# An attention layer with two expert layers: part-by-part order in every batch, ropes moved and cut, loads moved

## The chip, the cores and the metric

The kernel runs on one core of a Trainium2 chip. The metric is device time in microseconds (us), the median of the runs. A core has five engines with queues of their own, each executed in order: TensorE (PE; its weight loads are listed apart as PEld), VectorE (DVE), ScalarE (ACT), GpSimd (POOL) and the sync engine (SP), which here only issues DMAs.

## The reference

Four batches, eight heads, 576 positions, head size 64. After a rotation of q and k (the rope), scores, softmax and the product with v, the heads are laid side by side, and two expert layers follow: the first takes the maximum of three products and multiplies it by an output matrix, the second is a silu layer of width 2048.

```python
def rotate(x):
    x1, x2 = (x[..., :half], x[..., half:])
    return np.concatenate([x1 * cos - x2 * sin, x1 * sin + x2 * cos], axis=-1)
q_rot, k_rot = (rotate(q), rotate(k))
scores = scale * np.matmul(q_rot, k_rot.transpose(0, 1, 3, 2))
scores = scores - np.max(scores, axis=-1, keepdims=True)
attn = np.exp(scores)
attn = attn / (np.sum(attn, axis=-1, keepdims=True) + 1e-09)
attn_out = np.matmul(attn, v)
...
x = np.ascontiguousarray(attn_out.transpose(0, 2, 1, 3)).reshape(B * S, H * D)
h = np.maximum(np.maximum(x @ w1, x @ w2), x @ w3)
x = h @ w_out
h = x @ w_in
out = (h * (1.0 / (1.0 + np.exp(-h)))) @ w_out2
```

## The kernel before

**Attention tiles.** Heads are taken in pairs, four per batch. The 576 queries of a pair are five tiles: four of 128 rows and one of 64. `PARTS` calls tiles 0 and 1 the first part (256 queries) and tiles 2 to 4 the second (320). So there are 80 tiles, and the list `order` gives their sequence. In the first batch it goes through all four pairs' first parts and then through their second parts; in the other three it takes pair by pair, all five tiles of one before the next. A tile goes through scores on TensorE (lines 352 and 355), the negated row maximum on VectorE (362), exp on ScalarE (369), sum and reciprocal (379, 380), scaling on ScalarE (382), nine transposes on TensorE (398) with copies by ScalarE or VectorE (402, 404), and after each part of a pair the product with v (`av`, lines 413 and 417), which writes that pair's rows of x (420, 421).

**What comes ahead of a pair.** Its q and k are loaded into one of three raw buffers (`load_qk`), rotated in place (`qk_rope`: three instructions, lines 309, 310 and 313, with one work buffer w), and transposed (`qk_turn`, line 323), after which the raw buffer is free. A table `events` hangs these steps on tile numbers: `first[b, hp]` is a pair's first tile, and loads, ropes and turns stand so many tiles ahead of it. The rope of the first batch's pairs 0 and 1 is VectorE's, all others are GpSimd's.

**Filler.** The first expert layer (`moe1`, its matmuls in `group`, line 482) is a generator that the loop over the tiles draws on, some 8000 columns per tile. A batch is 576 matmuls of line 482: for each part 18 groups of 12 ("up") and 4 groups of 18 ("down"), with 256 columns in the first part and 320 in the second. `x_ready` says from which tile on a part of x may be used: the part must be whole for all four pairs. The last batch's matmuls come after the loop over the tiles, and the second expert layer after them. In the same loop the weights are made ready: W1's and WO1's pieces are loaded, narrowed (208, 210, 219, 220), measured, scaled and split in a high and a low half (`split`: GpSimd's line 155 and VectorE's 158, alternating piece by piece), and the second layer's weights are narrowed 256 columns at a time (205, 206, 219, 220).

**What sets the order.** The program order above is a priority; a scheduler with a timeline of its own then fixes every engine's queue, so instructions may move ahead of others. On the chip each queue runs in the fixed order.

## Time and profile before

| | us |
|---|---|
| median of 3 runs | 1127.57 (1127.56 to 1130.81) |
| the profiled execution | 1126.39 |
| its span, first to last instruction | 1124.7 |
| TensorE busy | 1036.1 |
| VectorE, ScalarE, GpSimd busy | 584.1, 503.9, 238.7 |
| mean granted TensorE clock | 0.956 |

The attention runs from the first row maximum at 23.9 us to the last at 651.8; the second expert layer fills the time from about 736 us to the end. TensorE's busy time includes waits between pipelined matmuls, so a stretch in which it is busy throughout is only known to have no visible gap.

### The profile page before, as it was taken

The page shows a single profiled execution, that of the slowest core. Times are in us where ns is not written, and L with a number is a line of the kernel's source. Part 1 is how long each engine was busy: PE and PEld are TensorE (multiplying, and loading weights), DVE is VectorE, ACT ScalarE, POOL GpSimd, SP SyncE. Part 2 cuts the span into 40 slices and gives each one's busy share as a digit, 9 for nine tenths or more (in the row PEclk, how much of TensorE's full clock was granted, in tenths as well). Part 3 has the DMA queues.
Part 4 walks back from the last instruction along what each step waited for, and adds up shares of the span by engine and source line. Part 5 has one row for each costly group of instructions (what it writes and reads, how often), then busy time and mean ns, then how long its engine had stood idle before and what let it go on. Part 6 is the DMA issues. An engine that isn't in the chain of part 4 may idle for free.

```text
span 1124.7 us, 16293 instructions
## 1 busy us (share of the span) xinstructions
PE 1036.1 (92%) x6250; PEld 632.7 (56%) x6250; DVE 584.1 (52%) x1102; ACT 503.9 (45%) x1200; POOL 238.7 (21%) x189
## 2 busy tenths in 40 slices
PE   2477898999978999999999997999999999999997
PEld 2244574666646776656776666654444444444554
DVE  4967667444477656566756549623444213423322
ACT  3567685555766676666767632121212002202111
POOL 3875113112134414332211106300000000000000
PEclk9687797899988999999999999999999999999999
DMA  7633021102332342232233136000101010100000
GB/s 191 187 106 116 17 68 51 51 2 59 98 102 87 107 121 86 60 96 71 85 92 93 54 131 264 15 24 1 38 29 47 13 26 1 29 29 1 19 20 19
DMA packets 79390, 76.10 MB, mean 68 GB/s; under 512 B 44752, under 2 KB 61648, under 8 KB 78288
## 3 DMA queue, kind: packets, MB, share of 16 engines
q1 hardware_dynamic: 75760, 65.03, 19.3%
q10 hardware_dynamic: 3552, 10.03, 2.7%
q8 instruction: 49, 0.80, 0.3%
q14 instruction: 29, 0.24, 0.1%
HBM read 57.21 MB, written 17.83 MB: 67 GB/s over the span
## 4 chain that ended last, share of the span: by engine, by line
PE 78%; DVE 5%; issue 2%; POOL 2%; ACT 2%; DMA 1%; SPq 0%; DVEq 0%; POOLq 0%; ACTq 0%
PE m L482 39%; PE o L726 17%; PE s L355 7%; PE tr L398 6%; PE xp L417 5%; PE s L352 2%; PE xp L413 1%; POOL wi L155 1%; DVE wi L158 1%; PE tr L323 1%; DVE z L219 1%; ACT e L382 1%; DVE nb L362 0%; DMA yr<-yscr 0%; POOL z L206 0%
## 5 line engine op out<-in xcount | busy, mean ns | idle before, releaser
L482 PE MATMUL m<-x,w 128*128 128x320 f16 (+1 forms) x1632 | 232.3, 290 | 9.1 <-DVE t L500 2.6
L726 PE MATMUL o<-wo,g 128*128 128x512 f16 x828 | 193.2, 379 | 0.0
L482 PEld LDWEIGHTS <-w 128*128 128x128 f16 x1632 | 157.5, 99 | 62.6 <-issue 20.9
L482 PE MATMUL m<-yt,wi 128*128 128x512 f16 (+1 forms) x920 | 189.8, 358 | 0.0
L712 ACT ACTIVATE gt<-m,ch 128x512 f32<-128x512 f32 (+1 forms) x80 | 51.5, 644 | 297.0 <-PE m L482 282.7
L362 DVE TENSOR_REDUCE nb<-s 128x2 f32<-128x1152 f32 (+1 forms) x80 | 108.2, 1352 | 64.8 <-PE s L355 64.7
L726 PEld LDWEIGHTS <-g 128*128 128x128 f16 x864 | 84.5, 98 | 99.7
L482 PEld LDWEIGHTS <-wi 128*128 128x128 f16 x920 | 89.6, 98 | 89.4
L369 ACT ACTIVATE e<-s,nb 128x576 f32<-128x576 f32 (+1 forms) x160 | 116.6, 734 | 50.6 <-DVE nb L362 49.6
L398 PE MATMUL tr<-ident,e 128*128 128x128 f32 (+1 forms) x720 | 118.7, 287 | 20.0 <-ACT pt L402 9.5
L382 ACT ACTIVATE e<-e,rec 128x576 f32<-128x576 f32 (+1 forms) x160 | 115.0, 767 | 23.7 <-DVE rec L380 23.6
L157 DVE TENSOR_SCALAR g<-gt,sg 128x512 f16<-128x512 f32 (+1 forms) x80 | 36.7, 459 | 162.8 <-ACT gt L712 162.8
L398 PEld LDWEIGHTS tr<-ident,e 128*128 128x128 f32 (+1 forms) x720 | 84.1, 149 | 50.9 <-ACT pt L402 14.7
L355 PE MATMUL s<-T 64*128 64x512 f32 (+5 forms) x480 | 109.3, 531 | 0.0
L206 POOL TENSOR_SCALAR z<-z 128x256 uint16<-128x256 uint16 x64 | 53.4, 834 | 211.1 <-DVE z L205 208.9
L417 PE MATMUL xp<-pt,vd 128*64 128x256 f32 (+1 forms) x512 | 90.7, 433 | 0.0
L402 ACT ACTIVATE pt<-tr 128x384 f32<-128x384 f32 (+1 forms) x160 | 70.3, 453 | 41.8 <-PE tr L398 41.2
L355 PEld LDWEIGHTS s<-T 64*128 64x128 f32 (+1 forms) x480 | 56.3, 192 | 38.5 <-issue 19.6
L482 PE MATMUL m<-h,wo 128*128 128x256 f16 (+1 forms) x512 | 72.8, 287 | 0.0
L500 DVE SCALAR_TENSOR_TENSOR t<-m,t 128x256 f32<-128x256 f32 (+1 forms) x96 | 43.5, 454 | 50.0 <-PE m L482 44.9
L309 POOL TENSOR_TENSOR w<-qk,sin_sb 128x1152 f32<-128x1152 f32 x14 | 37.5, 2676 | 128.5 <-DMA qk<-in_k_dram 103.7
L417 PEld LDWEIGHTS xp<-pt,vd 128*64 128x64 f32 x512 | 38.4, 141 | 37.5 <-issue 21.1
(158 smaller groups left out, 1090.8 us busy)
## 6 DMA issues: line engine op xcount, KB each, us to landing
z<-in_moe_w_in_dram SPq DMA_DIRECT2D x32, 256.0 KB, 2.9
z<-in_moe_w_out_dram SPq DMA_DIRECT2D x32, 256.0 KB, 3.0
w<-in_moe_w_dram ACTq DMA_DIRECT2D x6, 768.0 KB, 7.7
wo<-in_moe_w_dram ACTq DMA_DIRECT2D x6, 768.0 KB, 4.8
qk<-in_q_dram SPq DMA_DIRECT2D x32, 128.0 KB, 3.2
qk<-in_k_dram SPq DMA_DIRECT2D x32, 128.0 KB, 3.1
vd<-in_v_dram SPq DMA_DIRECT2D x16, 256.0 KB, 2.8
zwi<-z SPq DMA_DIRECT2D x32, 128.0 KB, 2.9
```

The source lines that it names most:

```text
L206: nc.gpsimd.tensor_scalar(out=q[:, :, 2], in0=q[:, :, 1], scalar1=step, scalar2=off, op0=ALU.mult, op1=ALU.add)
L355: nc.tensor.matmul(s[0:n, o:o + m], qs[r], kt[r, a:a + m], start=True, stop=True)
L362: x = nc.vector.tensor_reduce(out=nb[0:n], in_=s[0:n, 0:1152].rearrange("p (h k) -> p h k", h=2), op=ALU.max, axis=AX.X, negate=True)
L369: x = nc.scalar.activation(out=e[0:n, HK[g]], in_=s[0:n, HK[g]], func=AF.Exp, bias=nb[0:n, g:g + 1], accum_out=sm[0:n, g:g + 1])
L382: nc.scalar.activation(out=e[0:n, HK[g]], in_=e[0:n, HK[g]], func=AF.Copy, scale=r[0:n, g:g + 1])
L398: nc.tensor.transpose(tr[:, i * n:(i + 1) * n], e[0:n, c * P:(c + 1) * P], ident[0:n, 0:n])
L402: nc.scalar.activation(out=to, in_=of, func=AF.Copy)
L417: nc.tensor.matmul(xp[r, 0:n], v4[:, g, c, :], pt[:, c + 5 * g, :], start=False, stop=(c == 3))
L482: nc.tensor.matmul(ps[:, 0:n], l, r, start=(i == 0), stop=(i == len(passes) - 1))
L500: nc.vector.scalar_tensor_tensor(out=t, in0=ps[:, 0:n], scalar=2.0 ** -22, in1=part[-1], op0=ALU.mult, op1=ALU.max)
L712: nc.scalar.activation(out=gt, in_=ps[:, 0:n], func=AF.Silu, scale=ch)
L726: nc.tensor.matmul(ps, l, r, start=(f == 0 and i == 0), stop=(f == NF2 - 1 and i == 2))
```

## The change

It has four edits. `order` goes through the first parts of all pairs and then the second parts in every batch, so a batch's first part of x is whole after 8 tiles instead of 17. With this the first tiles of a batch's pairs stand two tiles apart instead of five, and the loads, ropes and turns that hang on them come closer together: a batch's first pair is loaded 12 tiles ahead of its first tile, the fourth 7 tiles ahead of the third pair's first tile, and the ropes stand 6 tiles ahead instead of 5. In the first batch VectorE does all four ropes. A rope on GpSimd is done in three chunks of 6 of the 18 blocks of columns, nine instructions of 128x384 instead of three of 128x1152. And the third and fourth v loads of batches 2 and 3 come 4 tiles ahead of the batch. Line numbers after the rope are higher by 2 or 3 in the changed kernel.

```diff
--- before.py
+++ after.py
@@ -304,13 +304,16 @@
         t = raw_t[b, hp]
         w = w_p.tile([P, 18, D], F32, tag="w", name="w")
         tt = (eng or nc.gpsimd).tensor_tensor
-        t4, w4 = (x.rearrange("p (a h) d -> p a h d", h=2) for x in (t, w))
-        sin2, cos2 = (x.unsqueeze(2).to_broadcast([P, 9, 2, D]) for x in (sin_sb, cos_sb))
-        tt(out=w4, in0=t4, in1=sin2, op=ALU.mult)
-        tt(out=t4, in0=t4, in1=cos2, op=ALU.mult)
-        u4 = t.rearrange("p a (t e) -> p a t e", t=2)
-        w4 = w.rearrange("p a (t e) -> p a t e", t=2)
-        return tt(out=u4, in0=u4, in1=w4[:, :, ::-1, :], op=ALU.add)
+        for lo, hi in ((0, 18),) if eng else ((0, 6), (6, 12), (12, 18)):
+            r, v = t[:, lo:hi, :], w[:, lo:hi, :]
+            t4, w4 = (x.rearrange("p (a h) d -> p a h d", h=2) for x in (r, v))
+            sin2, cos2 = (x[:, lo // 2:hi // 2, :].unsqueeze(2).to_broadcast([P, (hi - lo) // 2, 2, D]) for x in (sin_sb, cos_sb))
+            tt(out=w4, in0=t4, in1=sin2, op=ALU.mult)
+            tt(out=t4, in0=t4, in1=cos2, op=ALU.mult)
+            u4 = r.rearrange("p a (t e) -> p a t e", t=2)
+            w4 = v.rearrange("p a (t e) -> p a t e", t=2)
+            x = tt(out=u4, in0=u4, in1=w4[:, :, ::-1, :], op=ALU.add)
+        return x
 
     def qk_turn(b, hp):
 
@@ -427,8 +430,7 @@
 
 
     PARTS = [(0, 256, (0, 1)), (256, 320, (2, 3, 4))]
-    order = [(0, hp, r) for r in range(2) for hp in range(NP)]
-    order += [(b, hp, r) for b in range(1, B) for hp in range(NP) for r in range(2)]
+    order = [(b, hp, r) for b in range(B) for r in range(2) for hp in range(NP)]
     tiles, events, first, x_ready = [], {}, {}, {}
 
     def at(j, f, *a):
@@ -442,15 +444,15 @@
     for i, (b, hp) in enumerate(pairs):
         u = first[b, hp]
         if i > 2:
-            at(first[pairs[i - 1]] - 9 if i != 4 else 8, load_qk, b, hp)
+            at(first[pairs[i - 1]] - (7 if hp == 3 else 9) if hp or i < 4 else first[b, hp] - 12, load_qk, b, hp)
         if i == 0:
             continue
-        at(u - 5 if i > 3 else i - 4, qk_rope, b, hp, nc.vector if i == 1 else None)
+        at(u - 6 if i > 3 else i - 4, qk_rope, b, hp, nc.vector if i < 4 else None)
         at(u - 3, qk_turn, b, hp)
     for b in range(1, B):
         u = first[b, 0]
         for hp in range(NP):
-            at(u - 10 + hp if hp < 2 or b > 1 else u - 4, load_v, b, hp)
+            at(u - 10 + hp if hp < 2 else u - 4, load_v, b, hp)
             at(u - 2, v_max, b, hp)
         at(u, v_scale, b)
```

TensorE's queue at batch 1, pair 3, tiles 37 and 38 of the program: s is the scores' tile, tr a transposed tile, qk a raw buffer, xp the product with v. Before:

```order
L352 MATMUL s_2839<-kd_0_115,T_2554 128x128
L355 MATMUL s_2839<-T_2554 128x512
L355 MATMUL s_2839<-T_2554 128x384
L355 MATMUL s_2839<-T_2554 128x128
L398 MATMUL tr_2866<-ident_78,e_2743 128x128 x3
L323 MATMUL tr_2884<-ident_78,qk_2097 128x128 x4
L329 MATMUL tr_2896<-ident_78,qk_2097 128x128
L323 MATMUL tr_2890<-ident_78,qk_2097 128x128 x4
L352 MATMUL s_2911<-kd_0_115,T_2554 128x128
L355 MATMUL s_2911<-T_2554 128x512
L355 MATMUL s_2911<-T_2554 128x384
L355 MATMUL s_2911<-T_2554 128x128
```

At the same place, from tile 35, after (x_2020 is batch 1's x, m a group of the expert layer):

```order
L401 MATMUL tr_2840<-ident_78,e_2637 128x64 x3
L355 MATMUL s_2819<-kd_0_114,T_1777 128x128
L358 MATMUL s_2819<-T_1777 128x512
L358 MATMUL s_2819<-T_1777 128x384
L358 MATMUL s_2819<-T_1777 128x128
L484 LDWEIGHTS w_0_127
L484 MATMUL m_2875<-x_2020,w_0_127 128x256
L484 LDWEIGHTS w_0_127
L484 MATMUL m_2875<-x_2020,w_0_127 128x256
L484 LDWEIGHTS w_0_127
L484 MATMUL m_2875<-x_2020,w_0_127 128x256
L484 LDWEIGHTS w_0_127
```

Between the scores of two tiles there stood transposes alone; now the up matmuls of batch 1 stand there.

TensorE's queue at tiles 77 and 78, the last pair of the last batch. Before, from tile 77's scores (x_3548 is batch 2's x):

```order
L352 MATMUL s_6451<-kd_0_115,T_6138 128x128
L355 MATMUL s_6451<-T_6138 128x512
L355 MATMUL s_6451<-T_6138 128x384
L355 MATMUL s_6451<-T_6138 128x128
L398 MATMUL tr_6472<-ident_78,e_6290 128x64 x3
L482 LDWEIGHTS w_0_127
L482 MATMUL m_6517<-x_3548,w_0_127 128x320
L482 LDWEIGHTS w_0_127
L482 MATMUL m_6517<-x_3548,w_0_127 128x320
L482 LDWEIGHTS w_0_127
L482 MATMUL m_6517<-x_3548,w_0_127 128x320
L482 LDWEIGHTS w_0_127
```

After, from tile 77's scores through tile 78's:

```order
L355 MATMUL s_6708<-kd_0_115,T_5531 128x128
L358 MATMUL s_6708<-T_5531 128x512
L358 MATMUL s_6708<-T_5531 128x384
L358 MATMUL s_6708<-T_5531 128x128
L401 MATMUL tr_6734<-ident_78,e_6566 128x128 x3
L401 MATMUL tr_6763<-ident_78,e_6629 128x64 x3
L401 MATMUL tr_6773<-ident_78,e_6629 128x64 x3
L401 MATMUL tr_6768<-ident_78,e_6629 128x64 x3
L355 MATMUL s_6747<-kd_0_115,T_5531 128x128
L358 MATMUL s_6747<-T_5531 128x512
L358 MATMUL s_6747<-T_5531 128x384
L358 MATMUL s_6747<-T_5531 128x128
```

The expert matmuls that stood between these scores have gone ahead of them.

VectorE's queue at the start (nb is the row maximum, w a piece of W1 on line 219 and 220, qk_173 and qk_218 the raw buffers of pairs 2 and 3). Before:

```order
L313 TENSOR_TENSOR qk_153<-qk_153,w_221 128x1152
L362 TENSOR_REDUCE nb_264<-s_259 128x2
L219 TENSOR_SCALAR w_0_127<-w_0_127 128x768 x2
L327 COPY T_229<-tr_236 128x512
L220 SCALAR_TENSOR_TENSOR w_0_127<-w_0_251,w_0_127 128x768
L220 SCALAR_TENSOR_TENSOR w_0_127<-w_1_253,w_0_127 128x768
```

After:

```order
L315 TENSOR_TENSOR qk_153<-qk_153,w_214 128x1152
L311 TENSOR_TENSOR w_225<-qk_173,sin_sb_111 128x1152
L312 TENSOR_TENSOR qk_173<-qk_173,cos_sb_110 128x1152
L315 TENSOR_TENSOR qk_173<-qk_173,w_225 128x1152
L365 TENSOR_REDUCE nb_264<-s_259 128x2
L219 TENSOR_SCALAR w_0_127<-w_0_127 128x768 x2
L330 COPY T_229<-tr_236 128x512
L336 COPY kd_0_113<-tr_242 64x64 x2
L311 TENSOR_TENSOR w_247<-qk_218,sin_sb_111 128x1152
L220 SCALAR_TENSOR_TENSOR w_0_127<-w_0_251,w_0_127 128x768
L220 SCALAR_TENSOR_TENSOR w_0_127<-w_1_253,w_0_127 128x768
```

Pair 2's rope now stands ahead of the first row maximum, and pair 3's begins ahead of the second.

GpSimd's queue at the end of the first batch (wo_0 and wo1f are WO1's pieces; qk_1720 and qk_1380 are batch 1's fourth pair, qk_2097 and qk_2312 batch 2's first). Before:

```order
L309 TENSOR_TENSOR w_2416<-qk_1720,sin_sb_111 128x1152
L310 TENSOR_TENSOR qk_1720<-qk_1720,cos_sb_110 128x1152
L313 TENSOR_TENSOR qk_1720<-qk_1720,w_2416 128x1152
L155 TENSOR_SCALAR wo1f_129<-wo_0_130,swo1s_1544 128x512
L155 TENSOR_SCALAR wo_0_130<-wo_0_130,swo1s_1544 128x512 x2
L155 TENSOR_SCALAR wo_0_130<-wo_0_130,swo1b_1550 128x512 x3
L309 TENSOR_TENSOR w_2767<-qk_2097,sin_sb_111 128x1152
L310 TENSOR_TENSOR qk_2097<-qk_2097,cos_sb_110 128x1152
```

After:

```order
L315 TENSOR_TENSOR qk_1380<-qk_1380,w_1678 128x384 x2
L155 TENSOR_SCALAR wo1f_129<-wo_0_130,swo1s_1595 128x512
L311 TENSOR_TENSOR w_2756<-qk_2312,sin_sb_111 128x384
L155 TENSOR_SCALAR wo_0_130<-wo_0_130,swo1s_1595 128x512
L312 TENSOR_TENSOR qk_2312<-qk_2312,cos_sb_110 128x384
L311 TENSOR_TENSOR w_2756<-qk_2312,sin_sb_111 128x384 x2
L315 TENSOR_TENSOR qk_2312<-qk_2312,w_2756 128x384
L155 TENSOR_SCALAR wo_0_130<-wo_0_130,swo1s_1595 128x512
L312 TENSOR_TENSOR qk_2312<-qk_2312,cos_sb_110 128x384 x2
L155 TENSOR_SCALAR wo_0_130<-wo_0_130,swo1b_1601 128x512
L315 TENSOR_TENSOR qk_2312<-qk_2312,w_2756 128x384 x2
L155 TENSOR_SCALAR wo_0_130<-wo_0_130,swo1b_1601 128x512
```

The ropes of batch 2's first pairs now stand between WO1's splits, where they followed the last one.

## Rows read from the trace of the kernel before

**Rows 1.** the page, 40 slices: busy tenths of TensorE, its granted clock
```profile
PE   2477898999978999999999997999999999999997
...
PEclk9687797899988999999999999999999999999999
```
**Rows 2.** stretches: us, busy us (x instructions) by engine, clock, DMA
```profile
298.30:346.10 47.80, 36.66 (x209) 22.37 (x207) 34.68 (x69) 32.52 (x90) 21.80 (x16) 0.86 0.41 114
346.10:497.60 151.50, 150.60 (x1070) 105.33 (x1069) 89.72 (x199) 99.54 (x262) 44.43 (x33) 0.99 0.30 88
```
**Rows 3.** the same view, line 482 alone (expert matmuls)
```profile
298.30:346.10 47.80, 2.49 (x14) 1.53 (x15) 0.86 0.41 114
346.10:497.60 151.50, 80.39 (x573) 53.99 (x571) 0.99 0.30 88
497.60:506.40 8.80, 0.29 (x2) 0.23 (x3) 0.82 0.44 136
506.40:651.60 145.20, 77.95 (x554) 52.52 (x552) 0.99 0.26 79
```
**Rows 4.** the same view, line 362 alone (row maxima)
```profile
298.30:346.10 47.80, 9.47 (x7) 0.86 0.41 114
346.10:497.60 151.50, 25.70 (x19) 0.99 0.30 88
...
506.40:651.60 145.20, 25.73 (x19) 0.99 0.26 79
```
**Rows 5.** timeline of TensorE: start, us, instruction, xcount, idle before and its end
```profile
312.06 0.58 PE L398 MATMUL tr<-ident,e 64*128 64x64 f32 x3 [2.41 <-ACT pt L402]
```
**Rows 6.** timeline of TensorE after the attention
```profile
702.99 1.91 PE L482 MATMUL m<-h,wo 128*128 128x256 f16 x16
...
714.25 19.05 PE L482 MATMUL m<-x,w 128*128 128x320 f16 x139
```
**Rows 7.** timeline of VectorE in the first hole
```profile
326.57 1.36 DVE L362 TENSOR_REDUCE nb<-s 128x2 f32<-128x1152 f32 x1
...
331.18 1.36 DVE L362 TENSOR_REDUCE nb<-s 128x2 f32<-128x1152 f32 x1 [0.38 <-PE s L355]
```
**Rows 8.** timeline of GpSimd in the first batch
```profile
33.45 2.64 POOL L309 TENSOR_TENSOR w<-qk,sin_sb 128x1152 f32<-128x1152 f32 x1 [2.37 <-DMA qk<-in_k_dram]
```
**Rows 9.** timeline of VectorE, GpSimd idle beside these three
```profile
13.08 1.36 DVE L309 TENSOR_TENSOR w<-qk,sin_sb 128x1152 f32<-128x1152 f32 x1 [11.91 <-DMA qk<-in_q_dram]
...
93.87 0.54 DVE L219 TENSOR_SCALAR w<-w 128x768 int32<-128x768 int32 x1
...
94.80 0.94 DVE L220 SCALAR_TENSOR_TENSOR w<-wo,w 128x768 int32<-128x768 int32 x1
```
**Rows 10.** groups of VectorE from 22 to 62 us
```profile
L219 DVE TENSOR_SCALAR w<-w 128x768 int32<-128x768 int32 x6 | 9.8, 1659 | 0.0
L220 DVE SCALAR_TENSOR_TENSOR w<-w,w 128x768 int32<-128x768 int32 x4 | 9.2, 2323 | 0.0
L220 DVE SCALAR_TENSOR_TENSOR w<-wo,w 128x768 int32<-128x768 int32 x2 | 5.1, 2579 | 0.0
```
**Rows 11.** timeline of GpSimd, then of VectorE, end of the first batch
```profile
177.83 2.63 POOL L309 TENSOR_TENSOR w<-qk,sin_sb 128x1152 f32<-128x1152 f32 x1 [4.47 <-DMA qk<-in_k_dram]
...
183.31 2.70 POOL L313 TENSOR_TENSOR qk<-qk,w 128x1152 f32<-128x1152 f32 x1
...
177.88 2.87 DVE L507 TENSOR_TENSOR h<-t,h 128x256 f16<-128x256 f32 x1
...
183.60 2.95 DVE L220 SCALAR_TENSOR_TENSOR wo<-w,wo 128x512 int32<-128x512 int32 x1
```
**Rows 12.** timeline of GpSimd: first and last WO1 split, the next rope
```profile
193.90 0.69 POOL L155 TENSOR_SCALAR wo1f<-wo,swo1s 128x512 f16<-128x512 f32 x1 [7.90 <-DVE swo1i L128]
...
204.46 0.69 POOL L155 TENSOR_SCALAR wo<-wo,swo1b 128x512 f16<-128x512 f32 x1 [2.89 <-DVE wo L158]
222.21 2.63 POOL L309 TENSOR_TENSOR w<-qk,sin_sb 128x1152 f32<-128x1152 f32 x1 [17.06 <-DMA qk<-in_k_dram]
```

## The prediction

> **What bounds the kernel now.** Read the slices of the span first: TensorE is at 9 tenths from slice 8 to the end, with 7 or 8 left in a few places, and its granted clock dips in the same places [rows 1]. So the kernel is TensorE's work plus the stretches in which it can't work. The dips are told apart by the table of stretches, cut where the row maxima of attention tiles begin (tile numbers count the 80 tiles in program order). From 298.3 to 346.1 us TensorE has 36.66 us busy of 47.80 at a clock of 0.86; behind it, from 346.1 to 497.6, it has 150.60 of 151.50 [rows 2]. The same stretches counted by line 482, the matmuls of the expert layer, say why: 573 and 554 of them lie in the two long stretches, 14 and 2 in the two holes [rows 3]. The count of row maxima gives the tiles: 19 in each long stretch, 7 in the first hole [rows 4], one in the second. In a hole TensorE waits for the steps of one tile's chain, 2.41 us for a copy of the transposed tile in the row shown, and nothing else is in its queue [rows 5]. The hole is there because batches 1 to 3 run head pair by head pair: the first part of x is whole only when the last pair's first two tiles are done, at tile 17 of 20, and by then the previous batch's expert matmuls have run out.
>
> **Price of a tile, filled and unfilled.** An expert matmul costs 1.91 - 0.27 us over 15 steps, 0.109 us, with 256 columns, and 19.05 us over 139, 0.137 us, with 320 [rows 6]; a batch has 288 of each, so 0.123 us on average. The filled stretches hold 296.7 us, 38 tiles and 1127 such matmuls (138.6 us): (296.7 - 138.6) / 38 = 4.16 us per attention tile. The holes hold 56.6 us, 8 tiles and 16 matmuls (2.0 us): 6.83 us per tile. A tile without filler therefore wastes 2.67 us, and a tile is full from about 2.67 / 0.123 = 22 expert matmuls upward. This includes what the low clock in the holes costs.
>
> **Part 1, the order part by part.** After the change x's first part is whole at tile 8 of each batch, and 9 tiles earlier than before. In the new order of TensorE's queue no tile from 24 to 74 is empty: tiles 33 to 39 get 18 to 36 expert matmuls each (10 in all seven before, by the order), tile 59 gets 36, and the leanest, with 9 to 13, stand between fuller ones. The 8 unfilled tiles go: 8 x 2.67 = -21.4 us. The matmuls that fill them come from later, and since total TensorE work stays, the filler has to run out somewhere: the last three tiles. The new order gives tiles 75 to 79 16, 12, 0, 0 and 24 expert matmuls, where before 23 to 26 stood in each. Against the 22 that fill a tile that wastes 0.7 + 1.2 + 2.7 + 2.7 + 0 = +7.3 us. Bounds of this term: the holes hold GpSimd's ropes, 21.80 us of its time in the first [rows 2], and the last tiles have none; the quickest bare tile took 4.61 us, from 326.57 to 331.18 [rows 7], and at that price two bare tiles waste 0.9 and all of them about +1; if tile 79 and the drain behind it are bare too, 5 x 2.7 = +13. I take 7.3. Sum of part 1: -14 us (-20 to -8). What the last batch leaves for after the attention, and the layer after it, is the same work as before, so it stays.
>
> **Part 2, four ropes by VectorE in the first batch.** GpSimd loses the ropes of head pairs 2 and 3, six instructions of some 2.64 us [rows 8]; VectorE gains six of 1.36 us [rows 9], +8.2 us on an engine that from 22 to 62 us has hardly a gap. But it isn't busy with its own work there. Line 219 takes 1.66 us on average and line 220 2.32 and 2.58 [rows 10], against 0.54 and 0.94 when GpSimd is idle [rows 9]: 6 x 1.12 + 4 x 1.38 + 2 x 1.64 = 15.5 us of waiting. Roughly 9 us of it lies beside the two ropes that leave. So the two sides cancel, +8.2 - 9, with one addition: VectorE runs in order, and rope 3 now stands ahead of the second tile's row maximum. Its data is there only at about 33.4 us, where GpSimd's rope 3 starts after waiting for that DMA [rows 8]; VectorE would come to it near 30, so up to 3 us idle, with the maxima of tiles 0 and 1, and so all scores behind them, queued behind. Against that, GpSimd's queue is 17 us shorter when the W1 splits need it. I take -1 us, from -7 (all waiting goes) to +8 (none goes).
>
> Here a rule of the Trainium skill speaks against the change. In our rows a line 220 that starts at 183.60, while a GpSimd rope instruction holds from 183.31 to 186.01, takes 2.95 us and ends half a us after it [rows 11]; its own time with 512 elements is some 0.63, two thirds of the 0.94 for 768 [rows 9]. It waits out the other instruction. The Trainium skill, page SBUF - State Buffer, section Who interferes with whom, says that a VectorE instruction with two SBUF inputs and a GpSimd instruction that reads SBUF share a port pair as an exclusive lock, and that the second one to start blocks until the first is through; the row agrees. By that rule VectorE's own ropes, with two SBUF inputs, block behind GpSimd's line-210 instructions as well, which still run from 36 us on at some 2 us each: three instructions of rope 3 at up to 2 us would add up to 6 us to this term, which the upper bound above already holds.
>
> **Part 3, GpSimd's ropes in three chunks.** A rope instruction of 2.7 us [rows 11] becomes three; linear in size each is 0.9 us, and as GpSimd's instruction of 0.69 us with 512 elements shows [rows 12] a fixed part must be small, so 0.9 to 1.1. Nine instead of three make a rope at most 2 us longer on an engine that is busy for 44.43 of the 151.50 us of the filled stretch [rows 2]. The gain is VectorE's shorter wait: at 178 to 187 us two instructions on the way to WO1's scale take 2.87 and 2.95 us [rows 11] where about 0.6 is their own time, 4.6 us too much; with waits cut to a third, -3. The cost is in the same place: the new GpSimd order puts 12 chunks between the first and the last of WO1's six splits, some 12 us, where before 7.1 us of gaps lay (193.90 to 205.15 with 6 x 0.69 busy) [rows 12]; the down product needs the last split, so up to +5. I take -1, from -4 to +7. In the filled stretches TensorE sets the pace and the shorter waits give nothing.
>
> **Part 4, loads.** q/k loads are issued 7, 9 or 12 tiles ahead; only the fourth pair of a batch is short, since its raw buffer comes free with the first pair's turn. In the first batch it lands before 177.83, when its rope starts now [rows 11], and is turned some 30 us later in the new order: 9 chunks of 1 us fit. Loads of v for batches 2 and 3 move behind the av products that free their buffers. Cost 0, hidden by 4 tiles of 6.8 us; without that cover the turn on TensorE would wait.
>
> **Sum.** -14 - 1 - 1 = -16 us against the profiled execution's 1126.4 us (span 1124.7): 1110.4. That execution lies 1.2 us below the median of 1127.57 of the three timed runs, so 1111 to 1112; I say 1111.
>
> **Rivals.** (a) *The hole only moves.* The last five tiles are bare at the full price (+13 instead of +7.3) and VectorE's start costs +8: 1127 - 21 + 13 + 8 = 1127, within 0.3%. For it: the new order really has no expert matmul in tiles 77 and 78. Against it: VectorE's start must fail too. (b) *GpSimd's queue stops WO1.* The second split now stands behind the first chunk of batch 2's first rope, which needs that pair's q and k. Before, that rope waited 17.06 us for its DMA and started at 222.21, long after the last split [rows 12]. If the load lands as late as then, the split comes at 223 instead of 195.5, the down product's matmuls stand in order in TensorE's queue ahead of the next scores, and some 27 us are lost: 1111 + 27 = 1138, slower. In the new order of the sync queue the load stands ahead of the first y stores, which speaks for an earlier landing; the rival turns the result slower only from a landing near 211. (c) *VectorE's start is a loss* of 8 us: 1111 + 9 = 1120, still faster. By the Trainium skill's rule alone (SBUF - State Buffer) it would be 1111 + 1 + 6 = 1118. (d) *More than forecast*: GpSimd's free start pulls the whole first batch ahead by 7 us and the tail costs 2: 1099 to 1100. That the change doesn't do what it says is excluded by the order for the hole at tiles 33 to 39; whether filler costs as little there as elsewhere is the trace's to show.
>
> **How the numbers follow.** Forecast 0.55, (a) 0.12, (b) 0.08, (c) 0.15, (d) 0.10. 0.3% (about what a measurement of this kernel can tell from no change) is 3.4 us: faster is below 1124.2 and slower above 1131. Faster: 0.55 + 0.15 + 0.10 and a third of (a), 0.84. Same: the rest of (a) and a little of (b), 0.09. Slower: 0.07. The range from 1099 to 1122 holds the forecast's own bounds with (c) and (d), and leaves out (a) and (b), 0.2.
>
> **What would show it.** Right: from tile 23 to 74 no stretch of 40 us with a TensorE clock under 0.97; about 28 expert matmuls per tile in it; a new dip of TensorE over the last four tiles, some 20 us before the attention ends; line 220 beside a GpSimd rope at 1 to 1.9 us instead of 2.95; WO1's last split at 200 to 212. Wrong: filled tiles that cost more than 4.16 us plus their matmuls; the second row maximum after 40 us with no gain by tile 12; GpSimd idle before the second WO1 split for a q/k DMA.

## The result and the profile after

The changed kernel takes 1098.72 us (median of 4 runs, 1095.98 to 1101.79), the kernel before 1127.72 beside it: a ratio of 0.9737, 95% interval 0.9705 to 0.9769, or some 29 us. In two later comparisons it came to 0.9769 and 0.9764 (1103.06 and 1101.88 us). Faster was right. The 1111 us were 12 too many, and the range ended at 1099, 0.3 us above the first median.

The profiled execution has a span of 1098.0 us against 1124.7, with a mean TensorE clock of 0.978 against 0.956. The 40 slices of its page, TensorE's busy tenths and its granted clock, which answer to [rows 1]:

```profile
PE   2487899999998999999999988999999999999997
...
PEclk9789998999999999999999999999999999999999
```

The two low slices of TensorE, 11 and 12 counted from 0, have become one, slice 12, at 8 tenths. Most of the low clocks of slices 1 to 7 are gone, and these the prediction had not counted on. The next view is the table of stretches, cut at the row maxima of tiles 33, 40, 44, 75 and 79 (time, busy of TensorE, weight loads, VectorE, ScalarE, GpSimd, then clock and DMA), as in [rows 2]:

```profile
285.30:335.30 50.00, 48.81 (x359) 34.59 (x359) 36.68 (x77) 34.86 (x98) 17.15 (x19) 1.00 0.35 98
335.30:371.50 36.20, 32.88 (x221) 23.34 (x222) 21.49 (x52) 22.28 (x60) 21.88 (x24) 0.95 0.47 129
371.50:605.20 233.70, 232.10 (x1659) 162.90 (x1660) 142.41 (x320) 161.30 (x433) 55.60 (x62) 1.00 0.29 88
605.20:629.10 23.90, 21.97 (x133) 13.04 (x132) 13.29 (x33) 18.20 (x50) 3.21 (x4) 0.93 0.19 59
```

The same stretches for line 484 alone, the expert matmuls, as in [rows 3]:

```profile
285.30:335.30 50.00, 23.18 (x186) 17.52 (x186) 1.00 0.35 98
335.30:371.50 36.20, 16.03 (x114) 11.42 (x114) 0.95 0.47 129
...
605.20:629.10 23.90, 3.84 (x28) 2.58 (x28) 0.93 0.19 59
```

Tiles 33 to 39 take 50.0 us with 186 expert matmuls, where they took 47.8 with 14: the old hole is filled. But there are two places that lag now. The second row is new and was in no term: in tiles 40 to 43 the clock is 0.95 and 3.3 us of TensorE are idle. Before, these tiles took 30.0 us, with a clock of 0.94 and no idle time. The fourth is the tail that was forecast.

To see where the 26.7 us of the two spans lie, one cut is enough, the row maximum of tile 24, from which on every tile before the change has filler except the eight of the holes. It starts at 218.9 us before and at 206.5 after: 12.4 us lie ahead of it, and 14.3 behind it (905.8 against 891.5). The sum had put 2 ahead and 14 behind. The cut doesn't part exactly the same work: in the traces 299 expert matmuls start ahead of it before and 267 after, with 24 more transposes and 18 more matmuls of `av` in their place.

### The profile page after: what moved, and what is told of

It is laid out like the page before. It is cut to its first block, busy times and chain, and to the rows that moved or that the text cites. A ratio compares the mean times of both kernels' runs of the same rounds, so it can differ in the third digit from the quotient of the medians.

```text
span 1098.0 us, 16337 instructions
## 1 busy us (share of the span) xinstructions
PE 1019.9 (93%) x6250; PEld 625.9 (57%) x6250; DVE 568.4 (52%) x1108; ACT 501.0 (46%) x1200; POOL 242.3 (22%) x255
## 4 chain that ended last, share of the span: by engine, by line
PE 73%; DVE 5%; POOL 2%; DMA 1%; ACT 1%; issue 1%; DVEq 0%; SPq 0%; POOLq 0%
PE m L484 37%; PE o L728 17%; PE s L358 6%; PE tr L401 5%; PE xp L420 5%; PE s L355 1%; POOL wi L155 1%; PE xp L416 1%; PE tr L326 1%; DVE wi L158 1%; DVE nb L365 1%; DMA z<-in_moe_w_out_dram 1%; ACT e L372 1%; DVE vmax L145 1%; DVE wo L158 1%
## 5 line engine op out<-in xcount | busy, mean ns | idle before, releaser
L372 ACT ACTIVATE e<-s,nb 128x576 f32<-128x576 f32 (+1 forms) x160 | 116.6, 734 | 48.7 <-DVE nb L365 40.1
L401 PE MATMUL tr<-ident,e 128*128 128x128 f32 (+1 forms) x720 | 113.1, 273 | 16.0 <-ACT pt L405 6.9
L401 PEld LDWEIGHTS tr<-ident,e 128*128 128x128 f32 (+1 forms) x720 | 80.0, 142 | 41.9 <-ACT pt L405 10.8
L358 PE MATMUL s<-T 64*128 64x512 f32 (+5 forms) x480 | 103.0, 508 | 0.0
L405 ACT ACTIVATE pt<-tr 128x384 f32<-128x384 f32 (+1 forms) x160 | 70.2, 452 | 42.5 <-PE tr L401 41.7
L420 PE MATMUL xp<-pt,vd 128*64 128x256 f32 (+1 forms) x512 | 88.4, 422 | 0.0
L502 DVE SCALAR_TENSOR_TENSOR t<-m,t 128x256 f32<-128x256 f32 (+1 forms) x96 | 43.4, 452 | 48.8 <-PE m L484 48.0
L484 PEld LDWEIGHTS <-wo 128*128 128x128 f16 x512 | 49.2, 98 | 15.5 <-issue 3.1
```

Source lines behind the costliest of these rows:

```text
L358: nc.tensor.matmul(s[0:n, o:o + m], qs[r], kt[r, a:a + m], start=True, stop=True)
L372: x = nc.scalar.activation(out=e[0:n, HK[g]], in_=s[0:n, HK[g]], func=AF.Exp, bias=nb[0:n, g:g + 1], accum_out=sm[0:n, g:g + 1])
L401: nc.tensor.transpose(tr[:, i * n:(i + 1) * n], e[0:n, c * P:(c + 1) * P], ident[0:n, 0:n])
L405: nc.scalar.activation(out=to, in_=of, func=AF.Copy)
L420: nc.tensor.matmul(xp[r, 0:n], v4[:, g, c, :], pt[:, c + 5 * g, :], start=False, stop=(c == 3))
L484: nc.tensor.matmul(ps[:, 0:n], l, r, start=(i == 0), stop=(i == len(passes) - 1))
```

## Experiments

These are the theories for the difference. **A**: a VectorE instruction waits out the GpSimd instruction beside it, so the chunks carry the gain at the front. **B**: it is the emptier GpSimd queue, so VectorE's ropes carry it. **C** and **D** came up on the way: what the new order loses at tiles 40 to 43 is missing filler (C), or VectorE standing before a load of W2 (D). W2 stands for the weights of the second expert layer, whose pieces (tile z) are narrowed in the same loop. All kernels, with the two parts of the span (one profile each, so 2 to 4 us of scatter in the first part):

| kernel | median us | ratio to before, 95% interval | tile 24 at | from there on |
|---|---|---|---|---|
| before | 1127.7 to 1130.1 | | 218.9 | 905.8 |
| changed, three comparisons | 1098.72, 1103.06, 1101.88 | 0.9737, 0.9769, 0.9764 | 206.5, 210.2, 208.5 | 891.5, 891.6, 891.6 |
| vec_alone | 1129.37 | 1.0004, 0.9982 to 1.0025 | 225.2 | 902.0 |
| chunk_alone | 1108.51 | 0.9816, 0.9788 to 0.9844 | 204.1 | 900.2 |
| order_alone | 1119.44 | 0.9929, 0.9906 to 0.9952 | 220.7 | 904.3 |
| vec_chunk | 1108.84 | 0.9826, 0.9798 to 0.9853 | 206.5 | 900.4 |
| order_chunk | 1104.77 | 0.9790, 0.9759 to 0.9820 | 210.1 | 891.4 |
| order_vec | 1118.96 | 0.9907, 0.9875 to 0.9939 | 222.0 | 893.3 |
| chunk_from_7 | 1122.83 | 0.9941, 0.9917 to 0.9966 | 215.4 | 902.0 |
| chunk_to_6 | 1114.99 | 0.9867, 0.9830 to 0.9904 | 209.0 | 907.8 |
| chunk_nine | 1103.12 | 0.9766, 0.9746 to 0.9785 | 206.5 | 895.5 |
| late_ropes | 1103.12 | 0.9774, 0.9742 to 0.9806 | 209.1 | 891.3 |
| rate_7200 | 1109.67 | 0.9833, 0.9805 to 0.9861 | 201.8 | 906.1 |
| z_deeper, two comparisons | 1099.20, 1098.42 | 0.9735, 0.9740 | 208.9, 209.8 | 887.4, 887.5 |
| ahead_0 | 1104.58 | 0.9781, 0.9763 to 0.9799 | 210.0 | 892.3 |
| nine_z | 1104.23 | 0.9779, 0.9747 to 0.9810 | 211.3 | 893.3 |
| order_nine_z | 1103.34 | 0.9776, 0.9742 to 0.9810 | 204.9 | 897.0 |

The profiled execution of order_alone (span 1125.0) lies 7 us above its median; nothing rests on its last two columns. The columns of vec_alone don't compare with those of before either: 339 expert matmuls start ahead of its tile 24, 40 more than in before, some 4 us of work that is missing behind the cut.

### One part at a time

vec_alone, the kernel before with

```diff
-        at(u - 5 if i > 3 else i - 4, qk_rope, b, hp, nc.vector if i == 1 else None)
+        at(u - 5 if i > 3 else i - 4, qk_rope, b, hp, nc.vector if i < 4 else None)
```

> The kernel before with one change: four ropes by VectorE in the first batch (GpSimd's stay whole, the order stays). Theory A (GpSimd's long instructions hold VectorE up, so the chunks carry the gain at the front): VectorE's ropes are worth little by themselves, tile 4 begins some 2 us later as in the changed kernel (72.0 against 69.9 us), time 1124 to 1131. Theory B (an earlier and emptier GpSimd queue carries it): tile 12 begins 10 us or more earlier, time 1113 to 1118.

chunk_alone, the kernel before with the rope of the changed kernel:

```diff
+        for lo, hi in ((0, 18),) if eng else ((0, 6), (6, 12), (12, 18)):
+            r, v = t[:, lo:hi, :], w[:, lo:hi, :]
...
```

> The kernel before with one change: GpSimd's ropes in three chunks. Theory A: the splits of line 158 beside ropes at 76 to 93 us fall from 2.1 to 3.4 us to 1.0 to 1.9 us, the TensorE clock between 90 and 132 us stays higher, tile 12 begins 8 to 13 us earlier than at 132.1; time 1112 to 1119. Theory B: the splits get shorter but the front stays, tile 12 within 4 us; time 1122 to 1127.

order_alone, the changed kernel with the rope of before and `nc.vector if i == 1 else None` (the moved loads are still in it, so what is called the order from here on is order and loads together):

> The changed kernel with whole GpSimd ropes and only the second pair's rope by VectorE: the order part by part and the loads alone. Both theories: the holes at tiles 33 to 39 and 59 are gone, a new one at tiles 76 to 79, the front up to tile 12 as before within 3 us; -13 us as the changed kernel shows between tile 24 and tile 79 and behind it, so 1112 to 1117. Rival: part of the gain behind tile 24 in the changed kernel comes from the chunks, then 1118 to 1123.

order_chunk, the changed kernel with `nc.vector if i == 1 else None` alone:

> The changed kernel with only the second pair's rope by VectorE (order and chunks, without part 2). Theory A: nearly all of the gain, 1098 to 1104. Theory B: the gain at the front is lost, 1110 to 1115.

VectorE's ropes by themselves give nothing (ratio 1.0004), the order gives 0.7% (8 us), the chunks 1.8% (21 us), more than theory A had for them (1108.51 us for 1112 to 1119). B falls. order_alone, at 1119.44, came as its rival said and not at 1112 to 1117, and order_chunk, at 1104.77, just above A's range. What the chunks do is seen in lines 219 and 220, the groups of VectorE from 22 to 62 us that answer to [rows 10] (busy, mean ns of one). The changed kernel:

```profile
L219 DVE TENSOR_SCALAR w<-w 128x768 int32<-128x768 int32 x6 | 6.3, 1079 | 0.0
L220 DVE SCALAR_TENSOR_TENSOR w<-w,w 128x768 int32<-128x768 int32 x4 | 4.6, 1181 | 0.0
L220 DVE SCALAR_TENSOR_TENSOR w<-wo,w 128x768 int32<-128x768 int32 x2 | 3.4, 1758 | 0.0
```

vec_alone, the same groups:

```profile
L220 DVE SCALAR_TENSOR_TENSOR w<-w,w 128x768 int32<-128x768 int32 x4 | 7.9, 1995 | 0.0
L219 DVE TENSOR_SCALAR w<-w 128x768 int32<-128x768 int32 x6 | 7.0, 1194 | 0.0
L220 DVE SCALAR_TENSOR_TENSOR w<-wo,w 128x768 int32<-128x768 int32 x2 | 5.1, 2571 | 0.0
```

chunk_alone:

```profile
L219 DVE TENSOR_SCALAR w<-w 128x768 int32<-128x768 int32 x6 | 6.9, 1169 | 2.6 <-ACT w L208 2.6
L220 DVE SCALAR_TENSOR_TENSOR w<-w,w 128x768 int32<-128x768 int32 x4 | 4.7, 1203 | 3.3 <-POOL w L210 3.3
L220 DVE SCALAR_TENSOR_TENSOR w<-wo,w 128x768 int32<-128x768 int32 x2 | 2.9, 1438 | 0.0
```

The twelve instructions take 24.1 us before [rows 10], 20.0 with VectorE's ropes, 14.5 with chunks and 14.3 with both. Undisturbed they would take 8.9 (6 x 0.54 + 6 x 0.94, [rows 9]). The two ropes that leave GpSimd take only 4.1 us of waiting with them. GpSimd is idle in their place at first, but from 39 us on line 210's instructions stand beside VectorE's as before, and the next whole rope comes forward (its first instruction starts at 47.18 us in vec_alone, at 51.01 before). VectorE pays 8.2 us of rope work for it, and in the changed kernel its queue stands for that rope's load, as the timeline of VectorE shows:

```profile
31.56 1.36 DVE L311 TENSOR_TENSOR w<-qk,sin_sb 128x1152 f32<-128x1152 f32 x1 [2.32 <-DMA qk<-in_k_dram]
```

So tile 4 starts at 78.6 us in vec_alone and at 63.0 in chunk_alone, against 69.9 before. By tile 12 vec_alone has made up for it (131.0 against 132.1), and chunk_alone is at 123.8.

The second place is the low part of W1's splits, line 158. The timeline of VectorE before, between 80 and 93 us, beside whole ropes on GpSimd:

```profile
80.49 3.37 DVE L158 SCALAR_TENSOR_TENSOR w<-w,sw10s 128x768 f16<-128x768 f32 x1 [0.51 <-POOL w L155]
...
85.91 2.36 DVE L158 SCALAR_TENSOR_TENSOR w<-w,sw10s 128x768 f16<-128x768 f32 x1
...
90.61 2.06 DVE L158 SCALAR_TENSOR_TENSOR w<-w,sw10s 128x768 f16<-128x768 f32 x1
```

The same three in the changed kernel, the first two beside chunks:

```profile
79.37 1.75 DVE L158 SCALAR_TENSOR_TENSOR w<-w,sw10s 128x768 f16<-128x768 f32 x1
...
85.66 1.85 DVE L158 SCALAR_TENSOR_TENSOR w<-w,sw10s 128x768 f16<-128x768 f32 x1
...
89.58 1.00 DVE L158 SCALAR_TENSOR_TENSOR w<-w,sw10s 128x768 f16<-128x768 f32 x1
```

An undisturbed one takes 1.00: 4.8 us of waiting have become 1.6. TensorE's clock doesn't follow the chunks here: from 84 to 132 us it is 0.75 before and 0.96 in the changed kernel, but 0.82 in chunk_alone, 0.75 in chunk_to_6 below, which has the same chunks in these ropes, and 0.86 in vec_alone, which has none.

Between the profiles of before and chunk_alone lie 20.4 us: 6.9 up to tile 4, 8.8 in tiles 18 to 23 (47.3 against 38.5), 5.6 from tile 24 on, and 0.9 lost again in between.

### Where the chunks work, and how short they should be

chunk_from_7 and chunk_to_6, the kernel before with chunks in a part of the ropes:

```diff
-        for lo, hi in ((0, 18),) if eng else ((0, 6), (6, 12), (12, 18)):
+        for lo, hi in ((0, 18),) if eng or pairs.index((b, hp)) < 7 else ((0, 6), (6, 12), (12, 18)):
```

and `> 6` instead of `< 7` (the lines are shown against the rope of the changed kernel).

> The kernel before with chunks only in the ropes from the eighth pair on (index 7), whose first rope runs at 178 to 186 us; the five ropes at 22 to 92 us stay whole. By the accounts of the traces the chunks alone won 7 us up to tile 4 and 11 us in tiles 18 to 23, the latter with a TensorE clock of 1.00 instead of 0.72 from 172 to 208 us. Theory E (the two places stand by themselves): front as before (tile 12 within 2 us of 132.1), tiles 18 to 23 take some 38 us instead of 47, time 1115 to 1121. Rival (the clock in tiles 18 to 21 was a chance of the run, or rests on what came before): tiles 18 to 23 keep their 47 us, time 1124 to 1130.

> The kernel before with chunks only in GpSimd's ropes of pairs 2 to 6, which run at 22 to 92 us; from the eighth pair on they are whole. Chunks everywhere gave -20.8 us, from the eighth pair on alone -6.5. Theory F (the two places add up): front as with chunks everywhere (tile 12 at about 124), time about -14 to the kernel before, 1112 to 1118. Rival (tiles 18 to 23 gain only because the front is early, and chunks there give nothing of their own): the whole -18 to -21, 1108 to 1111.

The two add up, as theory F had it: -0.6% and -1.3% against -1.8% for both. For the later ropes alone neither E nor its rival held: 1122.83 us lies between their ranges, and tiles 18 to 23 took 44.0 us instead of 47.3, not 38. The stretch from 172 to 208 us, in before, chunk_from_7, chunk_to_6 and chunk_alone, shows what happens there:

```profile
172.00:208.00 36.00, 30.59 (x144) 17.35 (x142) 26.68 (x52) 18.42 (x46) 13.49 (x10) 0.72 0.12 30
```

```profile
172.00:208.00 36.00, 31.64 (x170) 18.55 (x168) 26.69 (x54) 19.73 (x49) 14.96 (x16) 0.81 0.14 34
```

```profile
172.00:208.00 36.00, 30.78 (x195) 20.84 (x193) 24.68 (x50) 23.74 (x58) 12.57 (x10) 0.91 0.17 45
```

```profile
172.00:208.00 36.00, 32.80 (x231) 22.88 (x229) 24.42 (x52) 26.84 (x66) 19.10 (x21) 1.00 0.18 48
```

TensorE is busy about as long in all four, but does 144, 170, 195 and 231 matmuls in it, with a mean clock of 0.72, 0.81, 0.91 and 1.00, a mix of its two levels of 1.2 and 2.4 GHz. TensorE's idle time in it, 5.4, 4.4, 5.2 and 3.2 us, doesn't go with the clock step by step, and only 2.3 of the 5.4 us before end with an instruction of VectorE (3.1 with one of ScalarE). That the clock, and not what is queued at another time, makes the difference is not shown: vec_alone, with whole ropes, has 0.91 and 200 matmuls in the same 36 us, yet takes 48.8 us for tiles 18 to 23. I could not set the clock.

chunk_nine, the kernel before with the changed kernel's rope and `[(x, x + 2) for x in range(0, 18, 2)]` as its chunks:

> The kernel before with GpSimd's ropes in nine chunks of 128 elements instead of three of 384. Theory A (VectorE waits out one GpSimd instruction at a time): the excess of VectorE's instructions up to tile 4, 16.1 us whole and 5.5 with three chunks, falls to 2 to 3; time as with three chunks or up to 4 us less, 1104 to 1110. Rival (27 instructions for a rope cost GpSimd too much in fixed parts, and the ropes come late): slower than with three chunks, 1112 to 1122.

The twelve instructions of lines 219 and 220 fall to 11.5 us, and VectorE's excess up to tile 4 (each duration less that of the fastest quarter of its form) to between 2 and 3 us, as A says. The time falls to 0.9766, as good as the changed kernel. Line 158 takes 1.20 or 1.21 us beside these chunks, as the timeline of VectorE shows:

```profile
80.15 1.21 DVE L158 SCALAR_TENSOR_TENSOR w<-w,sw10s 128x768 f16<-128x768 f32 x1 [0.93 <-POOL w L155]
```

But tile 4 starts no earlier (64.4), and tile 24 at 206.5, so the front seems to have another limit by then. The gain lies behind tile 24 (895.5 against chunk_alone's 900.2). The bare tiles 33 to 39 of the old order, those with hardly any filler, take 41.7 us with nine chunks and 47.8 to 48.7 with whole ropes (before, vec_alone, chunk_to_6). With three chunks they take 42.9, 44.8 and 46.8 (vec_chunk, chunk_alone, chunk_from_7), so that the step from three to nine lies there is not clear of the scatter.

late_ropes, the changed kernel with the ropes of pairs 4 to 6 queued on GpSimd behind W1's splits:

```diff
+    def late_rope(b, hp, eng=None):
+        with tc.issue_after(last["split"]):
+            qk_rope(b, hp, eng)
...
-        at(u - 6 if i > 3 else i - 4, qk_rope, b, hp, nc.vector if i < 4 else None)
+        at(2 * i + 2 if 3 < i < 7 else u - 6 if i > 3 else i - 4, late_rope if 3 < i < 7 else qk_rope, b, hp, nc.vector if i < 4 else None)
```

> The changed kernel, with GpSimd's ropes of pairs 4 to 6 (batch 1, not needed before tile 20) queued behind W1's splits instead of ahead of them; same instructions, other place. Theory A (a VectorE instruction waits out the GpSimd instruction beside it): VectorE's excess over the undisturbed durations up to tile 4, 7.2 us in the changed kernel, falls under 3, tile 12 begins 3 to 6 us earlier than at 118.7; time 1092 to 1098. Rival (the front is bound by the loads and VectorE's own work, the waits lie beside others): tile 12 within 1.5 us, time 1097 to 1102.

(`last["split"]` is the last split that was given to GpSimd.) The waiting moved with the ropes: up to tile 4 VectorE's excess fell from between 7 and 8 us (after_again) to under 4 and tile 4 starts 3.7 us earlier (69.6 against 73.3), but tile 12 at 118.4 against 120.2, and the time is the same (1103.12, 1103.06 beside it). The rival was nearer. Work of GpSimd that is only put elsewhere finds VectorE there too.

### What the order is worth

> The kernel before with VectorE's four ropes and GpSimd's chunks, but in the old order of parts. Theory C (with the holes' 12 us won at tiles 33 to 39, the new order loses nearly as much at tiles 20 to 24, 40 to 43 and in the tail): only some 3 us slower than the changed kernel, 1100 to 1106; the holes at tiles 33 to 39 and 59 are there. Rival (the order is worth the 14 us that the sum gave it, and vec and chunk overlap): 1108 to 1114.

> The changed kernel with whole ropes by GpSimd (order, loads and VectorE's four ropes, no chunks). Theory (the three parts add up: order -8, VectorE's ropes 0): 1118 to 1124. Rival (VectorE's ropes earn only where the chunks are missing, since they too take GpSimd's ropes out of VectorE's way): 1110 to 1117.

vec_chunk (the kernel before with both rope edits) is at 0.9826, no better than chunk_alone. Its 1108.84 us lie in the rival's range, but the changed kernel beside it took 1103.06, so the order is worth 5.8 us there and not the rival's 14. order_vec (the changed kernel with whole ropes) is at 0.9907, as its theory had it. So the order is worth 0.7% on top of both rope edits (0.9826 to the mean of the changed kernel's three, 0.9757), 0.3% on chunks alone, 0.7% by itself, 1.0% on VectorE's ropes: 3 to 11 us, and not 14. From tile 24 on it gives some 9 us: 900.2 to 891.4, 900.4 to 891.5, 902.0 to 893.3. The first pair is the cleanest: 299 and 285 expert matmuls start ahead of the cut in it, 299 and 267 in the second, 339 and 271 in the third, so that the three agree so well is in part chance. Up to tile 24 it costs 6.0 us on chunks alone (204.1 to 210.1) and some 2 on both (206.5 to a mean of 208.4).

For the second part I took, for each stretch, the time less the work in TensorE's queue: the number of its matmuls of each kind, as the kernel queues them, times the median from start to start of that kind in the trace of before (0.109 us for 256 columns of an expert matmul, 0.136 for 320, 0.109 for a transposition). What remains is lost time, an estimate: counted by the matmuls that start in each stretch of the traces, and with shorter times for the short ones, the differences between its rows move by up to 3 us (the changed kernel's 7.4 us over before at tiles 40 to 43 become about 5).

| tiles | 18 to 23 | 33 to 39 | 40 to 43 | 44 to 57 | 58, 59 | 75 to 78 | 79 to the end |
|---|---|---|---|---|---|---|---|
| before | 20.3 | 24.6 | 5.4 | 16.5 | 6.6 | 4.2 | 18.8 |
| vec_chunk | 14.2 | 19.4 | 4.5 | 14.8 | 11.4 | 4.2 | 19.0 |
| changed | 15.5 | 9.0 | 12.8 | 12.0 | 3.8 | 8.0 | 19.9 |

The holes at tiles 33 to 39 and 58, 59 give 18.0 us against vec_chunk. 8.3 of them are lost again at tiles 40 to 43 and 3.8 in the tail.

after_again and after_five, the changed kernel itself beside the others:

> The changed kernel itself, on the same chip as the three that go with it. 1096 to 1102, as in its own runs.

> The changed kernel once more, beside the one with the fourth buffer. 1098 to 1104.

rate_7200, ahead_0 and z_deeper, the changed kernel with one of

```diff
-    RATE = 8000
+    RATE = 7200
...
-        ahead = int(b > 0)
+        ahead = 0
...
-    z64_p = right("z64_p", 3)
+    z64_p = right("z64_p", 4)
```

> The changed kernel with 7200 instead of 8000 columns of expert matmuls per tile: the filler lasts to the end of the attention (18 or more in each of the last six tiles) and to tiles 40 to 43 (24, 48, 20 and 41 instead of 12, 21, 9 and 54). Theory C: the losses of the new order at tiles 40 to 43 (8 us above the old order) and 75 to 79 (3 us) come from missing filler and go: 1088 to 1094. Rival D (at tiles 40 to 43 VectorE stands before a load of W2's pieces, and TensorE behind it, whatever filler there is): only the tail's 3 us, 1094 to 1098.

> The changed kernel, in which a batch's down product of the first part no longer stands behind the first up block of the second part (which isn't ready before tile 44): 60 instead of 42 expert matmuls in tiles 40 to 42, and 24 instead of 12 at tile 60. Theory C: 2 to 4 us below the changed kernel. Rival D: within 1.5 us of it.

> The changed kernel with four instead of three buffers for the raw pieces of W2; TensorE's order is the same word for word. Rival D of the run before (at tiles 39 to 42 VectorE's line 205 waits for a load that was issued late because its buffer was taken, and TensorE's transposes wait behind it): the waits on that load go, tiles 39 to 43 take 4 to 7 us less, time 4 to 7 us below the changed kernel's. Theory C (too few expert matmuls there): within 2 us of the changed kernel.

> The changed kernel with four instead of three buffers for W2's raw pieces, side by side with it. If the loads of W2 are a part of the loss at tiles 39 to 43: 1.5 to 4 us below after_five. Otherwise: within 1 us.

In rate_7200 tiles 40 to 43 lose 4.5 us instead of 12.6, as C said, and the attention's last tile starts 7.7 us earlier. Yet the kernel is 6.6 us slower, and both ranges were missed: the saved filler is done after the attention, where it waits for VectorE. The waits of TensorE from the last tile's row maximum for some 95 us (total, times, longest), in rate_7200 and in the changed kernel:

```profile
PE m L484 <- DVE t L502: 14.9, 9, 3.1
```

```profile
PE m L484 <- DVE t L502: 6.8, 7, 2.0
```

VectorE merges the expert matmuls' results there between the splits of W2, and stands behind GpSimd's half of these. Here filler paid only where TensorE would otherwise have waited. ahead_0 took 3.9 us from tiles 40 to 43 and gave it back in tiles 44 to 74 and behind the attention: no change.

z_deeper is the one with a gain: 0.9740 beside 0.9764 for the changed kernel in five rounds (3.5 us by the medians; the intervals, 0.9723 to 0.9757 and 0.9748 to 0.9779, overlap a little, and the changed kernel's first comparison, 0.9737, is as good), with 887.4 and 887.5 us from tile 24 on in both of its profiles against 891.5 and 891.6 (twice). The mechanism that it takes away is seen best in order_chunk. The timeline of VectorE, and behind it TensorE's:

```profile
345.80 0.29 DVE L205 TENSOR_SCALAR z<-z 128x256 f32<-128x256 f32 x1 [2.27 <-DMA z<-in_moe_w_in_dram]
346.01 0.68 DVE L330 COPY T<-tr 128x512 f32<-128x512 f32 x1
```

```profile
346.75 0.55 PE L401 MATMUL tr<-ident,e 128*128 128x128 f32 x3 [2.68 <-DVE T L330]
```

The same transposes in the changed kernel and in z_deeper:

```profile
339.16 0.55 PE L401 MATMUL tr<-ident,e 128*128 128x128 f32 x3 [1.29 <-DVE T L330]
```

```profile
340.68 0.55 PE L401 MATMUL tr<-ident,e 128*128 128x128 f32 x3 [0.27 <-DVE T L330]
```

VectorE waits for a piece of W2, the copy of the turned pair stands behind it, and TensorE's transposes stand behind the copy for want of a buffer. In the changed kernel the same place costs 1.29 us, in z_deeper 0.27. Of the 4 us, some 1.5 to 2 lie at tiles 40 to 43 and some 2.4 at tile 75 and behind it, where TensorE's clock was 1.00 in both profiles and 0.72 to 0.93 in the changed kernel's tiles 77 and 78; the buffer isn't needed for the latter, since order_chunk, with three buffers, has a clock of 1.00 there too and takes 490.5 us from tile 75 on, as z_deeper does (490.6 and 490.4; the changed kernel 492.5 to 492.9). Of the rest of the loss at tiles 40 to 43 more filler takes most away, as rate_7200 shows. A part is VectorE beside ropes again. The changed kernel's VectorE there, and the first GpSimd chunk beside it:

```profile
343.71 0.94 DVE L219 TENSOR_SCALAR z<-z 128x256 int32<-128x256 int32 x1
344.57 1.08 DVE L205 TENSOR_SCALAR z<-z 128x256 f32<-128x256 f32 x1
345.57 0.41 DVE L220 SCALAR_TENSOR_TENSOR z<-z,z 128x256 int32<-128x256 int32 x1
345.91 0.54 DVE L407 COPY pt<-tr 128x384 f32<-128x384 f32 x1
```

```profile
343.50 1.00 POOL L315 TENSOR_TENSOR qk<-qk,w 128x384 f32<-128x384 f32 x1
```

Lines 219 and 205 take 0.28 and 0.27 us elsewhere (at 336.61 and 337.01); the copy behind them is what TensorE waits 1.85 us for:

```profile
346.50 0.40 PE L401 MATMUL tr<-ident,e 64*128 64x64 f32 x3 [1.85 <-DVE pt L407]
```

The new order puts four ropes of a batch into 8 tiles, and GpSimd is busy for 21.88 of these 36.2 us.

nine_z and order_nine_z, the changed kernel and order_chunk with nine chunks and z_deeper's buffer:

> The changed kernel with nine chunks and four buffers for W2's pieces. Theory A: shorter chunks take another 3 to 6 us as they did in the old order (1103 against 1108.5), and the fourth buffer 1 to 3: 1092 to 1098. Rival (TensorE's order has 12, 6, 10 and 6 expert matmuls in tiles 21 to 24 instead of 12, 16, 8 and 30, since GpSimd's many chunks stand between WO1's splits): 1098 to 1104.

> The same with only the second pair's rope by VectorE. If VectorE's four ropes add nothing once GpSimd's are short, as the old order shows (1108.8 against 1108.5): as nine_z within 2 us. If they are worth the 2 to 6 us that they gave in the new order: 2 to 6 us above nine_z.

They are at 0.9779 and 0.9776, no better than the changed kernel: nine_z's 1104.23 us lie just above the rival's range, and order_nine_z's 1103.34 say that VectorE's four ropes add nothing with short chunks. A reason would be that what nine chunks give in the old order they took from its bare tiles, which the new order doesn't have; no run shows it. z_deeper is the quickest from tile 24 on, and in its whole time level with the changed kernel's first comparison.

## Why the prediction was wrong

The term that failed is part 3's -1 us for the chunks. They were worth 16 to 21 us in the four pairs of kernels that differ by them alone (chunk_alone, vec_chunk, order_chunk and the changed kernel against the same without chunks).

**Part 1, the order.** The mechanism was right: the holes are filled and the tail pays. That the pair of kernels shows 14.3 us from tile 24 on, for -14, is luck: 5.4 of them are the chunks' and VectorE's ropes' (905.8 to vec_chunk's 900.4), and the order's own share is some 9 behind the cut, and 3 to 11 of the whole time. Against before, the holes gave 18.4 us (24.6 + 6.6 less 9.0 + 3.8) where the sum had 21.4, and the tail cost 3.8 and 1.1 where it had 7.3. The step that failed in this part is the sentence that the leanest tiles "stand between fuller ones". Tiles 40 to 43 lose 5 to 7.4 us more than before: for their few expert matmuls, as rate_7200 shows, and because the ropes of a whole batch and the pieces of W2 meet on VectorE there (0.94 and 1.08 us for 0.28 and 0.27, and 1.5 to 2 us with the fourth buffer). Nothing in the sum asked what else is due in the tiles that the new order makes lean.

**Part 2, VectorE's ropes.** The total was right (0 measured, -1 forecast; in the new order they gave 2 to 4 us, with intervals that overlap), for a wrong reason. "Roughly 9 us of it lies beside the two ropes that leave" assumed that GpSimd has nothing else to put there; 4.1 us went. The wait for the load came as described, 2.32 us against "up to 3". The rule of the Trainium skill (SBUF — State Buffer, Who interferes with whom) would have had 1118 here by a loss of VectorE's. The runs didn't put it to the test in this place: VectorE's rope instructions took 1.34 to 1.36 us each in vec_alone and in the changed kernel, with GpSimd idle beside all but the last of the twelve, and that one had started first. The rule is borne out in another place, below.

**Part 3, the chunks: the main error.** The term was -1 (-4 to +7), and the chunks alone gave 21 us. The price of a wait was read at one place, 178 to 187 us, and the gain was counted there only. The same wait stood in the rows of part 2: 15.5 us at lines 219 and 220, of which the chunks took 9.6 (24.1 to 14.5), and another 4.8 at line 158, which no term counted. I had given the front's waiting to VectorE's ropes and then took it as spent. The place that was counted, tiles 18 to 23, gained 8.8 us in chunk_alone where the term had 3, and 5.6 us came from tile 24 on, where it had "the shorter waits give nothing". What TensorE's clock, 0.75 and 0.72 in the two stretches of the first batch before, adds to this stays open. The cost that I put against it came true in part: the six splits of WO1 now span 18.7 us instead of 10.6, 180.45 to 199.14 us, with chunks between them, as the timeline of GpSimd shows in the changed kernel:

```profile
180.45 0.69 POOL L155 TENSOR_SCALAR wo1f<-wo,swo1s 128x512 f16<-128x512 f32 x1 [3.36 <-DVE swo1i L128]
182.25 1.00 POOL L311 TENSOR_TENSOR w<-qk,sin_sb 128x384 f32<-128x384 f32 x1 [1.10 <-DMA qk<-in_q_dram]
...
199.14 0.69 POOL L155 TENSOR_SCALAR wo<-wo,swo1b 128x512 f16<-128x512 f32 x1
```

**Part 4, the loads.** Nothing contradicts the 0 for the q, k and v loads. No run has the loads moved without the order, so their own share isn't measured. What was missed is that a load which nobody moved, W2's, comes late at tile 39 or 40 (TensorE waits 1.29 us behind it in the changed kernel, 2.68 in order_chunk). Since the buffer alone was changed in z_deeper, and not the loads, how much of it is the q/k loads ahead of it in SyncE's queue stays open.

**The rivals.** (a) did not happen: the tail cost 4.9 us, not 13. (b) did not happen: GpSimd waits 1.10 us for that load, not 27. (c)'s loss of 8 us is there at tile 4 of vec_alone (78.6 against 69.9) and gone at tile 12. The case that came is nearest to (d), at 0.10: "the whole first batch ahead by 7 us and the tail costs 2". It was 12.4 and 4.9. What it names as the cause, GpSimd's free start, was not it.

**What would show it.** Right: a new dip over tiles 75 to 79; line 220 beside a chunk at 1.18 and 1.76 us; about 28 expert matmuls per tile; the second row maximum before 40 us (36.0). Off: WO1's last split at 199.14 for "200 to 212"; and a stretch with a clock of 0.95 between tiles 23 and 74, which was the sign for the loss that the sum lacked. A sign of being wrong came as well: the tiles from 24 to 74 cost some 4.27 us each beside their matmuls instead of 4.16 (398.7 us, 1472 expert matmuls at 0.123, 51 tiles), 5.5 in tiles 40 to 43.

## To carry to other kernels

When an edit shortens an instruction on an engine that another one waits out, count the waits in every stretch where the two meet (here by the mean of one form beside its undisturbed duration), and not only where the edit's reason lies. When filler is moved, list what else falls due in the tiles that become lean, and what the filler would meet where it ends up. Measure parts of a change alone: here the part that the description names first was worth 3 to 11 us, and the third one 16 to 21.

## What the runs showed of the hardware

VectorE waited out one GpSimd instruction at each of three lengths: line 158 took 2.06 to 3.37 us beside rope instructions of 2.63, 1.75 and 1.85 beside chunks of 1.00, and 1.20 or 1.21 with nine chunks, where 1.00 is its own time. This goes for line 219 too, which has one input in SBUF: 1.66 us on average beside whole ropes and line 210 [rows 10], 0.54 undisturbed [rows 9], and at 343.71 us in the changed kernel it ends 0.15 us after the chunk shown beside it. The Trainium skill, page SBUF — State Buffer, section Who interferes with whom, says so of VectorE instructions with two SBUF inputs, and of copies, casts and tensor_scalar in a two-port mode: the pair of ports is locked for the whole instruction. The rows agree. By that rule chunks of a third of the length would take two thirds of the waits beside ropes, an estimate; in rows it is 9.6 of 15.2 us (from 24.1 to 14.5, with 8.9 undisturbed), and some of these waits are beside line 210, which stayed whole.

A rope chunk of 128x384 takes 1.00 us where a third of 2.63 would be 0.88, so three chunks cost GpSimd 14% more time. I found no stretch that it decides.

TensorE's busy time hides its clock: over the same 36 us it did 144 matmuls at 0.72 and 231 at 1.00, while it was busy for 30.6 and 32.8 us. How much of a stretch's time the lower clock took is not parted from the waits by any run.
